# Converting half of the last part's weights inside the last part, and carrying W_out's second half through DRAM

## The chip, the cores and the metric

The kernel runs on one core of one Trainium2 chip. The metric is device time in microseconds (us), smaller is better. Three runs of the kernel before gave 1499.52, 1499.49 and 1498.40 us; their median, 1499.49 us, is the time to compare with. The profile is of one further execution.

## The reference, cut to what matters

Batch 8, 8 heads, sequence 576, head size 64, 32 memory slots; the weights and inputs arrive as 64-bit floats.

```
a = softmax of phi along the sequence
k_m, v_m = a^T k, a^T v                       # 32 memory slots for each head
x = softmax(q k_m^T / 8) v_m                  # 4608 tokens x 512
h = x @ w_in                                  # 512 -> 2048
x = (h - tanh(h)) @ w_out                     # 2048 -> 512
out = max(x @ w1, x @ w2, x @ w3) @ moe2_w_out   # 512 -> 768 -> 512
```

## The kernel before, in words

**Three stages.** The program computes the attention together with the tanh layer, and then the layer of three maxima, which is called the last part here. The tanh layer is cut into 16 blocks of 128 hidden units (`fc`). Blocks 0 to 7 are phase 0 and blocks 8 to 15 phase 1. In each phase the loop runs over tiles of 288 to 512 tokens, and within a tile over 8 blocks. One pass of that loop is a **step**: `emit_h` multiplies into PSUM (`ps_h`), `emit_g` makes `gh` = h - tanh(h) as a high and a low half (ScalarE `th`, VectorE L434, ScalarE cast L436, GpSimd L437), and `emit_x` multiplies `gh` by a block `wo` of W_out into `ps_x`, 12 matmuls. Phase 0 has 104 steps, phase 1 has 96; two batches take 24 steps of phase 1, and 24 of phase 0 after its first 32. The partial result goes to DRAM (`xd[0]`), and phase 1 adds its own share. Attention runs in the shadow of phase 0: generators for batches 2 to 7 are queued with due steps.

**Products.** Each product is three matmuls of high and low halves (`mm3`, L94 to L96), so each weight is needed as two 32-bit halves.

**Conversions.** `conv` (L113 to L138) turns 128 rows of 64-bit weights into those halves. It is one DMA into `raw` (two buffers), one ScalarE operation (L120), five VectorE operations (L122, L123, L125, L127, L128), one GpSimd addition (L134), one ScalarE cast into the high half (L135) and one GpSimd subtraction into the low half (L137). For w_in there is one half only, and one GpSimd addition (L131) ends it.

**What sets the order.** Two tracks (`Track`) hold generators, `fg` for attention and `bg` for conversions. `slot()` is called five times in a step and advances each track by `rate` quarters of a generator's step. An entry may have a gate, the first step at which it may move. On top of that the program's scheduler puts the instructions of each engine in an order of its own, so a conversion can stand earlier in an engine's queue than its place in the source. Every engine and each DMA queue works its instructions in that order.

**Which conversions stand where before the change.** W_out's blocks 0 to 7 and the first two quarters of w_in are converted at the start. The last part's weights (`last_w`: 24 pieces of W1 to W3 of 384 columns by `wb_conv`, 6 pieces of the last W_out by `wz_conv`) are converted from the first due step of batch 2 on, into one staging buffer `cs` (one copy only), and stored to DRAM: three DMAs for each `wb_conv` (L333), one for each `wz_conv` (L339). When attention is over and its memory is free, the third quarter of w_in (`wi2`) and W_out's blocks 8 to 15 (`wo1`) are converted, then the rest of `last_w`. In phase 1 the first two of six weight tiles `wb[j]` are loaded from DRAM (L591, GpSimd's queue), and at the start of the last part the other four (L608) and the six tiles `wz[j]` (L612).

**The last part.** Nine tiles of 512 tokens. For each, six groups `j`: `emit_max` runs 36 matmuls into three PSUM banks, ScalarE copies the first out (L624), VectorE takes two maxima (L625, L626), ScalarE and GpSimd split the result (`mh`, L628, L629). Each bank name has two buffers. From the second tile on `emit_out` is mixed in, 18 matmuls `ps_o` over all six `wz` for 128 tokens of the tile before. `split_x` prepares the next tile's input (`xr`, `xh`, L581, L582).

Of the kernel before, what the change touches and what calls it, by code (L numbers as in the profile page):

```python
# [22 lines left out]
def kernel(  # L23
# [26 lines left out]
    P = 128  # L50
# [62 lines left out]
    def conv(src, n, hi, lo=None):  # L113
        raw = cv_p.tile([P, 512, 2], U32, tag="raw", bufs=2, name="raw")
        DMA.dma_start(out=raw[:, :n].rearrange("p c t -> p (c t)"), in_=src.bitcast(U32))
        yield
        a = cv_p.tile([P, 512], U32, tag="cva", bufs=2, name="cva")[:, :n]
        b = cv_p.tile([P, 512], U32, tag="cvb", bufs=2, name="cvb")[:, :n]
        hw, lw = raw[:, :n, 1], raw[:, :n, 0]
# [205 lines left out]
    wb_d = [dram.tile([P, 3, KD, 2, P], F32, name=f"wb_d{j}") for j in range(J)]
    wz_d = [dram.tile([P, 2, DM], F32, name=f"wz_d{j}") for j in range(J)]

    def wb_conv(w, kc, g):
        t = cv_p.tile([P, 2, 512], F32R, tag="cs", bufs=1, name="cs")
# [4 lines left out]
        yield  # L334

    def wz_conv(j):
        t = cv_p.tile([P, 2, 512], F32R, tag="cs", bufs=1, name="cs")
        yield from conv(moe2_w_out[j * P:(j + 1) * P, :], DM, t[:, 0], t[:, 1])
        DMA.dma_start(out=wz_d[j], in_=f(t))  # L339
        yield  # L340
# [202 lines left out]
    for g in last_w:  # L543
        bg.add("last", g, start[0, 2])
# [68 lines left out]
    m_t = {}  # L613

    def emit_max(i, j):
# [7 lines left out]
        m = b_p.tile([P, NT], F32, tag="m", bufs=3, name="m")  # L623
# [8 lines left out]
    def emit_out(i, u):  # L632
        ps = ps_b.tile([P, DM], F32, tag="o", bufs=2, name="ps_o")
# [4 lines left out]
        ob = b_p.tile([P, DM], F32, tag="ob", bufs=3, name="ob")  # L638
# [50 lines left out]
```

## Time and profile before

| | before |
|---|---|
| median of three runs | 1499.49 us |
| the profiled execution | 1499.77 us |
| its span, first to last instruction | 1498.0 us |
| TensorE matmul (PE) busy | 1369.6 us, 91% |
| VectorE (DVE) busy | 645.1 us, 43% |
| GpSimd (POOL) busy | 461.5 us, 31% |
| ScalarE (ACT) busy | 419.8 us, 28% |
| mean granted TensorE clock | 0.975 |

PE is the matmul row, PEld its weight loads. A wait row says which engine's line waited for what: total us, how often, and the longest. SP issues most DMAs. "Landing" is the time from a DMA's issue to its completion.

The order of stages in the span is: start to 134 us, attention with phase 0 to 559, phase 1 to 897, the last part to the end.

### The profile page before, as it was taken

To read this page: it belongs to the slowest core of one execution; us is meant where nothing else is said; L and a number is where in the kernel's file an instruction comes from. 1 tells how busy PE (TensorE), PEld (TensorE's weight loads), DVE (VectorE), ACT (ScalarE), POOL (GpSimd) and SP (SyncE) were. 2 spreads that over 40 slices of the span, in tenths; PEclk is the share of its full clock that TensorE was granted. 3 is DMA by queue.
4 is the path that set the end of the run, shared out by engine and by line. 5 is a ranking of instruction groups with operands and counts; after the bars stand their busy time and mean duration, and the time that the engine had idled before them with its cause. 6 is when DMAs were issued, how large, how long until landed. Compare 5 with 4: busy or idle time off the path is not lost.

```text
span 1498.0 us, 21579 instructions
## 1 busy us (share of the span) xinstructions
PE 1369.6 (91%) x8672; PEld 1131.2 (76%) x8672; DVE 645.1 (43%) x1043; ACT 419.8 (28%) x817; POOL 461.5 (31%) x420
## 2 busy tenths in 40 slices
PE   2575988889998888999999999999999999999998
PEld 1354867677786666788898998888888888888887
DVE  3888787875447994642323222211212121211111
ACT  1323344343343353442323322111111111111110
POOL 0446555543335574543232332111111111111110
PEclk9977899999999998999999999999999999999999
DMA  8565878766432346642312227101101010110001
GB/s 208 142 192 142 230 214 233 210 173 162 120 118 79 129 157 207 209 155 78 113 47 85 75 73 272 36 15 46 46 14 43 15 47 17 43 35 15 15 14 43
DMA packets 190068, 159.75 MB, mean 107 GB/s; under 512 B 95248, under 2 KB 163856, under 8 KB 188176
## 3 DMA queue, kind: packets, MB, share of 16 engines
q1 hardware_dynamic: 188240, 145.79, 33.5%
q0 software_dynamic: 1728, 12.58, 2.3%
q8 instruction: 68, 1.11, 0.3%
q14 instruction: 32, 0.26, 0.1%
HBM read 105.64 MB, written 52.69 MB: 106 GB/s over the span
## 4 chain that ended last, share of the span: by engine, by line
PE 66%; DVE 13%; DMA 8%; SPq 5%; issue 3%; POOL 3%; ACT 2%; DVEq 0%; ACTq 0%; POOLq 0%
PE ps_w L96 10%; PE ps_w L95 10%; PE ps_w L94 10%; PE ps_x L94 5%; PE ps_x L95 5%; PE ps_x L96 5%; DMA wb_d<-cs 3%; PE ps_o L95 3%; PE ps_o L94 3%; PE ps_o L96 3%; PE ps_h L94 3%; PE ps_h L96 3%; PE ps_h L95 3%; DVE cvb L125 2%; SPq L176 2%
## 5 line engine op out<-in xcount | busy, mean ns | idle before, releaser
L437 POOL TENSOR_TENSOR gh<-th,gh 128x320 fp32r<-128x320 f32 (+2 forms) x200 | 209.7, 1050 | 320.3 <-ACT gh L436 311.4
L95 PE MATMUL ps_x<-gh,wo 128*128 128x320 f32 (+2 forms) x800 | 271.0, 341 | 6.7 <-POOL gh L437 6.5
L94 PE MATMUL ps_x<-gh,wo 128*128 128x320 f32 (+2 forms) x800 | 257.0, 343 | 11.8 <-ACT gh L436 6.6
L96 PE MATMUL ps_x<-gh,wo 128*128 128x320 f32 (+2 forms) x800 | 265.6, 335 | 0.7 <-POOL wo L137 0.7
L96 PE MATMUL ps_w<-xh,wb 128*128 128x512 f32 x648 | 255.0, 394 | 0.0
L95 PE MATMUL ps_w<-xh,wb 128*128 128x512 f32 x648 | 254.5, 393 | 0.0
L94 PE MATMUL ps_w<-xh,wb 128*128 128x512 f32 x648 | 253.9, 392 | 0.0
L629 POOL TENSOR_TENSOR mh<-m,mh 128x512 fp32r<-128x512 f32 x54 | 69.8, 1295 | 490.3 <-ACT mh L628 490.3
L434 DVE TENSOR_TENSOR th<-ps_h,th 128x320 f32<-128x320 f32 (+2 forms) x200 | 106.4, 534 | 197.8 <-ACT th L433 197.7
L94 PE MATMUL ps_h<-at,vw 128*128 128x320 f32 (+2 forms) x512 | 160.1, 313 | 32.5 <-DVE th L434 20.9
L94 PEld LDWEIGHTS ps_x<-gh,wo 128*128 128x128 f32 x800 | 150.8, 194 | 38.9 <-issue 17.7
L95 PEld LDWEIGHTS ps_x<-gh,wo 128*128 128x128 f32 x800 | 154.5, 193 | 27.9 <-POOL gh L437 14.5
L96 PEld LDWEIGHTS ps_x<-gh,wo 128*128 128x128 f32 x800 | 153.8, 193 | 10.9 <-issue 1.0
L625 DVE TENSOR_TENSOR m<-ps_w,m 128x512 f32<-128x512 f32 x54 | 37.3, 691 | 283.0 <-PE ps_w L96 283.0
L96 PE MATMUL ps_h<-at,vw 128*128 128x320 f32 (+2 forms) x512 | 155.5, 305 | 1.0 <-DVE vw L312 1.0
L95 PE MATMUL ps_h<-at,vw 128*128 128x320 f32 (+2 forms) x512 | 155.1, 303 | 0.0
L94 PEld LDWEIGHTS ps_h<-at,vw 128*128 128x128 f32 x512 | 100.4, 196 | 62.7 <-DVE th L434 35.6
L436 ACT CAST gh<-th 128x320 fp32r<-128x320 f32 (+2 forms) x200 | 99.7, 499 | 162.4 <-DVE th L434 150.6
L433 ACT ACTIVATE th<-ps_h 128x320 f32<-128x320 f32 (+2 forms) x200 | 94.8, 476 | 177.1 <-PE ps_h L96 168.8
L95 PEld LDWEIGHTS ps_w<-xh,wb 128*128 128x128 f32 x648 | 121.7, 188 | 27.8
L94 PEld LDWEIGHTS ps_w<-xh,wb 128*128 128x128 f32 x648 | 121.8, 188 | 27.5
L96 PEld LDWEIGHTS ps_w<-xh,wb 128*128 128x128 f32 x648 | 121.7, 188 | 27.1
(80 smaller groups left out, 1714.5 us busy)
## 6 DMA issues: line engine op xcount, KB each, us to landing
raw<-in_moe_w_out_dram SPq DMA_DIRECT2D x22, 512.0 KB, 3.5
qt<-in_q_dram SPq DMA_DIRECT2D x128, 72.0 KB, 3.0
at_d<-at SPq DMA_DIRECT2D x16, 576.0 KB, 3.5
raw<-in_moe_w_dram SPq DMA_DIRECT2D x24, 384.0 KB, 3.4
wb_d<-cs SPq DMA_DIRECT2D x72, 128.0 KB, 3.6
at<-at_d SPq DMA_DIRECT2D x8, 1152.0 KB, 5.6
wb<-wb_d POOLq DMA_DIRECT2D x6, 1536.0 KB, 9.3
xr<-xd SPq DMA_DIRECT2D x36, 256.0 KB, 2.9
```

The lines of the kernel that those rows point to most:

```text
L94: T.matmul(o, w[0], x[0], start=start, stop=False)
L95: T.matmul(o, w[0], x[1], start=False, stop=False)
L96: T.matmul(o, w[1], x[0], start=False, stop=stop)
L125: V.scalar_tensor_tensor(out=b, in0=hw, scalar=0xC0000000, in1=b, op0=ALU.bitwise_and, op1=ALU.bitwise_or)
L176: DMA.dma_start(out=t[64 * e + 32 * h:64 * e + 32 * h + 32, r], in_=src[e, h, r])
L433: S.activation(th, ps, AF.Tanh)
L434: V.tensor_sub(th, ps, th)
L436: S.copy(gh[:, 0], th)
L437: G.tensor_sub(gh[:, 1], th, f(gh[:, 0]))
L625: V.tensor_max(m, pss[1], m)
L629: G.tensor_sub(mh[:, 1], m, f(mh[:, 0]))
```

## The change

- `conv` loses the column count (it always takes 512 columns, now also as 4 x 128 of three-dimensional sources) and gets one `yield` more behind its DMA. Its buffers come from `cv[0]`, which is the last part's pool `b_p` once that is open.
- `wo_store` and `wo_load` are new: W_out's blocks 8 to 15 are converted from the first due step of batch 2 on, stored to DRAM (8 DMAs of 512 KB), and loaded into `wo1` when attention's memory is free.
- `wb_conv` takes one weight matrix and one `j` at a time, 512 x 128 entries. For j = 0 to 2 (nine conversions) it stages through `cs` and stores one DMA each, gated to phase 1. For j = 3 to 5 (nine) and for all six `wz` it writes straight into the last part's tiles while that part runs: `emit_max` steps the track six times ahead of each of its three products and then insists on what it needs.
- Of the loads at the start of the last part, one (`wb[2]`) stays. `m` and `ob` go from three to two buffers.

```diff
+    cv = [cv_p]
+    def conv(src, hi, lo=None):
+        raw = cv[0].tile([P, 512, 2], U32, tag="raw", bufs=2, name="raw")
...
+        yield
         yield
...
+    def wo_store(fc):
+        t = cv_p.tile([P, 2, DM], F32R, tag="cs", bufs=1, name="cs")
+        yield from conv(moe_w_out[(FC + fc) * P:(FC + fc + 1) * P, :], t[:, 0], t[:, 1])
+        DMA.dma_start(out=wo_d[fc], in_=f(t))
+        yield
+    def wo_load(fc):
+        t = wo_t[FC + fc] = wo1.tile([P, 2, DM], F32R, name=f"wo{FC + fc}")
+        DMA.dma_start(out=f(t), in_=wo_d[fc])
+        yield
+    JP = 3
+    def wb_conv(w, j, t=None):
+        o = cv_p.tile([P, KD, 2, P], F32R, tag="cs", bufs=1, name="cs") if t is None else t[:, w]
         src = (moe2_w1, moe2_w2, moe2_w3)[w]
-        yield from conv(src[kc * P:(kc + 1) * P, g * 384:(g + 1) * 384], 384, t[:, 0, :384], t[:, 1, :384])
-        for i in range(3):
-            DMA.dma_start(out=wb_d[3 * g + i][:, w, kc], in_=f(t[:, :, i * P:(i + 1) * P]))
+        yield from conv(src[:, j * P:(j + 1) * P].rearrange("(k p) c -> p k c", p=P), o[:, :, 0], o[:, :, 1])
+        if t is None:
+            DMA.dma_start(out=wb_d[j][:, w], in_=f(o))
+            yield
+    def wz_conv(j, t):
+        yield from conv(moe2_w_out[j * P:(j + 1) * P, :], t[:, 0], t[:, 1])
...
-    for g in last_w:
-        bg.add("last", g, start[0, 2])
+    for fc in range(FC):
+        bg.add("wos", wo_store(fc), start[0, 2])
...
-    bg.add("wo1", chain(*[wo_conv(fc, wo1) for fc in range(8, 16)]))
-    bg.q += rest
-    rate[1] = 8
+    bg.add("wo1", chain(*[wo_load(fc) for fc in range(FC)]))
+    for j in range(JP):
+        for w in range(3):
+            bg.add("wb", wb_conv(w, j), start[1, 0])
+    rate[1] = 6
...
+        if j < JP:
+            G.dma_start(out=wb[j], in_=wb_d[j])
+        else:
+            for w in range(3):
+                bg.add(("wb", j), wb_conv(w, j, wb[j]))
...
-        G.dma_start(out=wz[j], in_=wz_d[j])
+        bg.add("wz", wz_conv(j, wz[j]))
...
+        bg.need_all(("wb", j))
         for w in range(3):
+            for _ in range(LR):
+                bg.step(10 ** 9)
```

On VectorE, from the end of phase 1 into the last part, the kernel before has only the split of the next tile and the maxima (L465 is the last addition of phase 1, L582 the split, L625 and L626 the maxima):

```order
L465 TENSOR_TENSOR xo<-ps_x_8574,xo 128x320
L582 TENSOR_TENSOR xh<-xr,xh 128x512 x2
L625 TENSOR_TENSOR m<-ps_w_8799,m 128x512
L626 TENSOR_TENSOR m<-ps_w_8812,m 128x512
L625 TENSOR_TENSOR m<-ps_w_8845,m 128x512
L582 TENSOR_TENSOR xh<-xr,xh 128x512 x2
L626 TENSOR_TENSOR m<-ps_w_8858,m 128x512
```

In the changed kernel the same stretch of VectorE (L485, L602, L654 and L655 are now these lines; L126 to L132 are the five operations of a conversion):

```order
L485 TENSOR_TENSOR xo<-ps_x_8234,xo 128x320
L126 TENSOR_SCALAR cva<-cva 128x512
L127 TENSOR_SCALAR cvb<-cva 128x512
L129 SCALAR_TENSOR_TENSOR cvb<-raw,cvb 128x512
L126 TENSOR_SCALAR cva<-cva 128x512
L131 TENSOR_SCALAR cva<-cvb 128x512
L127 TENSOR_SCALAR cvb<-cva 128x512
L132 SCALAR_TENSOR_TENSOR cva<-raw,cva 128x512
L129 SCALAR_TENSOR_TENSOR cvb<-raw,cvb 128x512
L654 TENSOR_TENSOR m<-ps_w_8470,m 128x512
L602 TENSOR_TENSOR xh<-xr,xh 128x512 x2
```

Fifteen conversions, 75 such rows, stand between the end of phase 1 and the ninth pair of maxima.

On GpSimd, around the change from phase 0 to phase 1, the kernel before (L134 and L137 end a conversion, L437 is the step's own work, L591 the loads of `wb[0]` and `wb[1]`):

```order
L137 TENSOR_TENSOR wo_5465<-cva,wo_5465 128x512
L437 TENSOR_TENSOR gh<-th,gh 128x320
L134 TENSOR_TENSOR cva<-cvb,cva 128x384
L437 TENSOR_TENSOR gh<-th,gh 128x320
L137 TENSOR_TENSOR cs<-cva,cs 128x384
L134 TENSOR_TENSOR cva<-cvb,cva 128x384
L437 TENSOR_TENSOR gh<-th,gh 128x320
L591 DMA wb_5717<-wb_d_97 128x3072
L591 DMA wb_5718<-wb_d_98 128x3072
L134 TENSOR_TENSOR cva<-cvb,cva 128x384
L137 TENSOR_TENSOR cs<-cva,cs 128x384
```

The same place in the changed kernel (L138 and L142 end a conversion, L457 is the step's own work, L611 the loads):

```order
L142 TENSOR_TENSOR cs<-cva,cs 128x4x128
L138 TENSOR_TENSOR cva<-cvb,cva 128x512
L457 TENSOR_TENSOR gh<-th,gh 128x320 x2
L138 TENSOR_TENSOR cva<-cvb,cva 128x512
L142 TENSOR_TENSOR cs<-cva,cs 128x4x128
L611 DMA wb_5336<-wb_d_105 128x3072
L457 TENSOR_TENSOR gh<-th,gh 128x320 x3
L142 TENSOR_TENSOR cs<-cva,cs 128x4x128
```

The eight W_out conversions ahead of this place are gone, conversions of W1 to W3 stand there instead, staged through `cs`, and the two loads stand apart: `wb[1]` follows seven rows further down.

On ScalarE at the start of the last part the changed kernel has (L124 begins a conversion, L653 copies the first bank of a group out of PSUM, L140 casts a converted weight, L601 and L657 are the other casts):

```order
L124 ACTIVATE cva<-raw 128x512
L653 COPY m<-ps_w_8447 128x512
L124 ACTIVATE cva<-raw 128x512
L601 CAST xh<-xr 128x512 x2
L140 CAST wb_8428<-cva 128x4x128
L657 CAST mh<-m 128x512
L653 COPY m<-ps_w_8522 128x512
L140 CAST wb_8428<-cva 128x4x128
L124 ACTIVATE cva<-raw 128x512
```

The kernel before has L624, L581 and L628 there alone. The third conversion's first operation now stands behind the copy of the second group's first bank.

## Rows read from the trace of the kernel before

**Rows 1.** Windows: length; PE, PEld, DVE, ACT, POOL busy (count); clock; DMA share, GB/s

```profile
134.00:239.00 105.00, 89.66 (x890) 77.56 (x890) 82.88 (x150) 42.76 (x96) 59.10 (x59) 0.89 0.76 217
239.00:344.00 105.00, 94.00 (x896) 77.45 (x897) 80.91 (x135) 45.16 (x92) 55.92 (x52) 1.00 0.68 184
344.00:445.00 101.00, 96.62 (x956) 81.46 (x956) 54.32 (x94) 37.56 (x75) 35.38 (x33) 1.00 0.51 134
...
481.00:559.00 78.00, 66.20 (x369) 50.19 (x368) 74.01 (x96) 31.83 (x63) 50.03 (x40) 1.00 0.40 134
559.00:657.00 98.00, 88.91 (x548) 74.47 (x547) 57.73 (x97) 40.32 (x83) 51.22 (x46) 0.95 0.63 211
657.00:740.00 83.00, 83.00 (x539) 71.91 (x538) 23.65 (x44) 27.32 (x55) 24.38 (x24) 1.00 0.26 90
682.00:740.00 58.00, 58.00 (x364) 49.61 (x362) 15.99 (x29) 18.28 (x37) 16.54 (x16) 1.00 0.29 100
897.00:1498.00 601.00, 596.18 (x2596) 486.97 (x2594) 109.38 (x162) 92.83 (x158) 74.01 (x62) 1.00 0.15 46
```

**Rows 2.** Windows of the tile ps_x alone: PE, PEld, DVE, ACT busy (matmuls)

```profile
481.00:559.00 78.00, 41.43 (x192) 31.90 (x192) 1.35 (x2) 1.55 (x4) 1.00 0.40 134
...
682.00:740.00 58.00, 39.74 (x192) 31.85 (x192) 4.17 (x8) 0.00 (x0) 1.00 0.29 100
```

**Rows 3.** Waits of ACT, 130 to 345 and 445 to 660: total, times, longest

```profile
ACT cs L135 <- DMA wb_d<-cs: 36.6, 16, 5.1
...
ACT cs L135 <- DMA wb_d<-cs: 15.4, 3, 8.7
```

**Rows 4.** Groups by line and form, DVE, 481 to 559: busy us, mean ns

```profile
L125 DVE SCALAR_TENSOR_TENSOR cvb<-raw,cvb 128x512 uint32<-128x512 uint32 x13 | 15.7, 1211 | 0.3
L128 DVE SCALAR_TENSOR_TENSOR cva<-raw,cva 128x512 f32<-128x512 uint32 x13 | 10.8, 835 | 0.3
L127 DVE TENSOR_SCALAR cva<-cvb 128x512 uint32<-128x512 uint32 x13 | 10.6, 816 | 0.3
L123 DVE TENSOR_SCALAR cvb<-cva 128x512 uint32<-128x512 uint32 x12 | 10.5, 874 | 0.3
L122 DVE TENSOR_SCALAR cva<-cva 128x512 f32<-128x512 f32 x12 | 8.9, 739 | 2.6 <-ACT cva L120 2.6
```

**Rows 5.** The tiles cva and cvb, whole span: min/median/max ns

```profile
L122 DVE TENSOR_SCALAR cva<-cva x62: 343/428/1420, 30.0 to 632.3; 128x512 f32<-128x512 f32 x38, 128x384 f32<-128x384 f32 x24
L123 DVE TENSOR_SCALAR cvb<-cva x62: 301/426/1637, 30.4 to 633.0; 128x512 uint32<-128x512 uint32 x38, 128x384 uint32<-128x384 uint32 x24
...
L125 DVE SCALAR_TENSOR_TENSOR cvb<-raw,cvb x62: 503/691/1784, 30.9 to 634.6; 128x512 uint32<-128x512 uint32 x38, 128x384 uint32<-128x384 uint32 x24
L127 DVE TENSOR_SCALAR cva<-cvb x62: 341/426/1407, 32.2 to 635.6; 128x512 uint32<-128x512 uint32 x38, 128x384 uint32<-128x384 uint32 x24
L128 DVE SCALAR_TENSOR_TENSOR cva<-raw,cva x62: 508/692/1787, 32.9 to 636.7; 128x512 f32<-128x512 uint32 x38, 128x384 f32<-128x384 uint32 x24
```

**Rows 6.** Timeline of POOL and of DVE, 505 to 509: start, duration

```profile
506.41 1.47 POOL L134 TENSOR_TENSOR cva<-cvb,cva 128x512 f32<-128x512 f32 x1
...
506.77 1.40 DVE L123 TENSOR_SCALAR cvb<-cva 128x512 uint32<-128x512 uint32 x1
```

**Rows 7.** Groups by form, POOL and ACT, 481 to 559

```profile
L137 POOL TENSOR_TENSOR wo<-cva,wo 128x512 fp32r<-128x512 f32 x8 | 11.5, 1434 | 1.5 <-ACT wo L135 1.5
L134 POOL TENSOR_TENSOR cva<-cvb,cva 128x512 f32<-128x512 f32 x8 | 10.7, 1338 | 8.7 <-DVE cva L128 8.7
...
L135 ACT CAST wo<-cva 128x512 fp32r<-128x512 f32 x8 | 5.0, 619 | 6.2 <-POOL cva L134 6.1
```

**Rows 8.** Groups by form, DVE and POOL, the last part, 897 to the end

```profile
L625 DVE TENSOR_TENSOR m<-ps_w,m 128x512 f32<-128x512 f32 x54 | 37.3, 691 | 283.0 <-PE ps_w L96 283.0
...
L629 POOL TENSOR_TENSOR mh<-m,mh 128x512 fp32r<-128x512 f32 x54 | 69.8, 1295 | 490.3 <-ACT mh L628 490.3
```

**Rows 9.** DMA issues, whole span: KB each, median us to landing

```profile
wz_d<-cs SPq DMA_DIRECT2D x6, 512.0 KB, 3.1
```

More of the change, by code (lines that the diff above doesn't have):

```diff
@@ L110, in small @@
             tc.add_manual_dep(b, a.name, mybir.DependencyInfo(mybir.DependencyClass.NoSync, mybir.DependencyReason.DATA), reason="side by side")
[L113 to L115 removed]
+    cv = [cv_p]
+    def conv(src, hi, lo=None):
+        raw = cv[0].tile([P, 512, 2], U32, tag="raw", bufs=2, name="raw")
+        u = src.bitcast(U32)
+        DMA.dma_start(out=raw.rearrange("p (k c) t -> p k (c t)", k=u.shape[1]) if len(u.shape) == 3 else raw.rearrange("p c t -> p (c t)"), in_=u)
         yield
[L117 to L119 removed]
+        yield
+        a = cv[0].tile([P, 512], U32, tag="cva", bufs=2, name="cva")
+        b = cv[0].tile([P, 512], U32, tag="cvb", bufs=2, name="cvb")
+        hw, lw = raw[:, :, 1], raw[:, :, 0]
         S.activation(f(a), f(hw), AF.Abs)
@@ L134, in conv @@
         G.tensor_add(f(a), f(b), f(a))
-        S.copy(hi, f(a))
+        x = f(a).rearrange("p (k c) -> p k c", k=hi.shape[1]) if len(hi.shape) == 3 else f(a)
+        S.copy(hi, x)
         yield
-        G.tensor_sub(lo, f(a), f(hi))
+        G.tensor_sub(lo, x, f(hi))
         yield
@@ L145, in wi_conv @@
         for r in range(HP):
-            yield from conv(moe_w_in[r * P:(r + 1) * P, fq * FQ:(fq + 1) * FQ], FQ, t[:, r])
+            yield from conv(moe_w_in[r * P:(r + 1) * P, fq * FQ:(fq + 1) * FQ], t[:, r])
         wi[fq] = t
@@ L320, in wo_conv @@
         t = p.tile([P, 2, DM], F32R, name=f"wo{fc}")
-        yield from conv(moe_w_out[fc * P:(fc + 1) * P, :], DM, t[:, 0], t[:, 1])
+        yield from conv(moe_w_out[fc * P:(fc + 1) * P, :], t[:, 0], t[:, 1])
         wo_t[fc] = t
[L325 to L329, printed above, removed]
-        src = (moe2_w1, moe2_w2, moe2_w3)[w]
-        yield from conv(src[kc * P:(kc + 1) * P, g * 384:(g + 1) * 384], 384, t[:, 0, :384], t[:, 1, :384])
-        for i in range(3):
-            DMA.dma_start(out=wb_d[3 * g + i][:, w, kc], in_=f(t[:, :, i * P:(i + 1) * P]))
[L334 to L340, printed above, removed]
+    wo_d = [dram.tile([P, 2, DM], F32, name=f"wo_d{fc}") for fc in range(FC)]
+    def wo_store(fc):
[8 more added lines that the diff above has]
+    JP = 3
+    wb_d = [dram.tile([P, 3, KD, 2, P], F32, name=f"wb_d{j}") for j in range(JP)]
+    def wb_conv(w, j, t=None):
+        o = cv_p.tile([P, KD, 2, P], F32R, tag="cs", bufs=1, name="cs") if t is None else t[:, w]
+        src = (moe2_w1, moe2_w2, moe2_w3)[w]
+        yield from conv(src[:, j * P:(j + 1) * P].rearrange("(k p) c -> p k c", p=P), o[:, :, 0], o[:, :, 1])
[4 more added lines that the diff above has]
+        yield from conv(moe2_w_out[j * P:(j + 1) * P, :], t[:, 0], t[:, 1])
     class Track:
@@ L366, in need, with need_all @@
                         break
+        def need_all(self, name):
+            while any(x[0] == name for x in self.q):
+                self.need(name)
     fg, bg = Track(), Track()
@@ L622, in emit_max @@
             pss.append(ps)
-        m = b_p.tile([P, NT], F32, tag="m", bufs=3, name="m")
+        m = b_p.tile([P, NT], F32, tag="m", bufs=2, name="m")
         S.copy(m, pss[0])
@@ L637, in emit_out @@
             mm3(ps, (mh[:, 0, o], mh[:, 1, o]), (wz[j][:, 0], wz[j][:, 1]), j == 0, j == J - 1)
-        ob = b_p.tile([P, DM], F32, tag="ob", bufs=3, name="ob")
+        ob = b_p.tile([P, DM], F32, tag="ob", bufs=2, name="ob")
         (S.copy if u % 2 else V.tensor_copy)(ob, ps)
```

8 lines of the change are left out of this document (4 added, 4 removed).

## The prediction

> **What bounds the kernel now.** I read the windows by stage first: in which stretch is PE (TensorE's matmul row) short of the stretch, and which engine is full there. From 897 to the end PE is busy 596.2 of 601 us at full clock [rows 1]. The last part is bound by its matmuls, so nothing taken from it is worth anything there, and whatever makes PE wait adds to the time. In phase 1, once the conversions are over, PE is busy 83.0 of 83.0 us for 24 steps (657 to 740), and 58.0 of 58.0 for the 16 steps from 682 [rows 1]. These two are my floors. The stretches that are longer than their floors all hold conversions:
>
> - 481 to 559, the last 16 steps of phase 0, takes 78 us. It has the same 192 matmuls into `ps_x` as the 58 us from 682 [rows 2]. DVE (VectorE) is busy 74.0 of the 78 [rows 1]: it is the bound.
> - 559 to 657, the first 24 steps of phase 1, takes 98 us against 83, with the granted clock at 0.95 [rows 1]. The waits of ACT (ScalarE) show one of 8.7 us for the store of `cs` [rows 3]; it stands beside the loads of `wb[0]` and `wb[1]`.
> - 239 to 344 takes 105 us, 344 to 445 takes 101 [rows 1], both for 24 steps with two batches of attention. The first holds ten conversions, the second none. So with attention beside them the conversions cost 4 us in 105, not more.
>
> **What one conversion costs.** On DVE between 481 and 559 the five operations average 1.211, 0.835, 0.816, 0.874 and 0.739 us [rows 4], together 4.5 us. Their medians over the whole span are 0.43, 0.43, 0.69, 0.43 and 0.69, together 2.7 [rows 5]. The difference is waiting for POOL (GpSimd): a 0.43 us operation that starts at 506.77 takes 1.40 us and ends about when POOL's addition of 506.41 ends [rows 6]. POOL itself spends 1.34 + 1.43 = 2.8 us on a conversion [rows 7].
>
> **The change, stretch by stretch.** The conversions stay the same number of weights: 62 before (24 of them of 384 columns), 56 after, all of 512. What matters is where they stand on DVE.
>
> 1. *134 to 344, gain 6 us (0 to 10).* The instruction order has 9 conversions where 12 stood up to 239, and 2 where 10 stood from 239 to 344. For the second piece the difference between the two equal stretches bounds the gain at 4 us [rows 1]; I take 3. In the first piece DVE has the same work within a few us, since 512 columns cost more than 384; what falls away is two thirds of the stores of `cs`. ACT waited 16 times, 36.6 us in all, for them between 130 and 345 [rows 3], with `th` and `gh` of the coming steps queued behind. I take 3.
> 2. *481 to 559, gain 10 us (4 to 16).* There are 12 conversions in these steps instead of 15: the eight of W_out are now loads, six of W1 to W3 move in from later, and of w_in two have their DVE part done long before. Three at 4.5 us are 13.4 us off a DVE that is 95% busy; the floor, 58 us, is not reached. I take back 3 us, because the six go through the one `cs`: cast 0.6 and subtraction 1.4 [rows 7], landing 3.1 [rows 9] and the issue ahead of it make between 5 and 6 us each, in some 40 us. The eight new loads of W_out, 4 MB, sit in SP's queue right behind attention's last store near 480 and are needed from 559 on. At 3.1 us for a transfer of that size [rows 9] they take 25 us even one after the other, and are there about 50 us early: nothing.
> 3. *559 to 657, gain 9 us (2 to 14).* Of the 15 us over the floor 8.7 are that one wait, and 0.05 of 98 us, about 5, the lower clock. After the change a store of `cs` still stands directly ahead of the load of `wb[0]`, but `wb[1]` comes seven rows later, so half as many bytes stand in the way at once: I leave half of the wait and none of the clock's loss. Three or four conversions follow here instead of nine or ten.
> 4. *657 to 897: nothing.* No conversion stood here and none does now.
> 5. *The last part, loss 11 us (0 to 25).* Fifteen conversions now run beside matmuls that have no slack. Its 2592 matmuls take 601 us [rows 1], 0.232 each, so a group `j` takes PE 36 x 0.232 = 8.35 us. In the changed order the product that needs the last converted tile comes after 343 matmuls, 79.6 us into the part, near 976.9. DVE starts after phase 1's last additions, near 898.3, and has before it: 15 x 4.475 = 67.1 us of conversions, 16 maxima at 0.691 [rows 8] = 11.1, four splits of about the same length = 2.8, and about 5 us of waiting for `xr`'s DMA and for ACT at the start. That is 984.3; POOL's addition, ACT's cast and POOL's subtraction add 3.4, so 987.7. PE waits 10.8 us in all. I take the 4.5 us because POOL is about as busy as between 481 and 559, where it was 50.0 of 78 [rows 1]: 15 x 2.8 plus eight `mh` at 1.295 [rows 8] are 52 in 88 us. The tail's 3.4 us are 1.34, 0.62 and 1.43 [rows 7]. At 2.7 us a conversion is hidden, that is the low end. If DVE and POOL took strict turns, 2.7 + 2.8 = 5.4 us, it would be 81.5 for the conversions, 10.4 for `mh`, 2.8, 5 and 3.4 on top of 898.3, so 24.5 us late: the high end. ACT, busy 92.8 of the 601 us [rows 1], has room for its two operations a conversion, and three loads of `wb` and six of `wz` fall away from POOL's queue; they were hidden.
> 6. *The clock, loss 2 us (0 to 8).* With PE idle 11 of 105 us the granted clock stayed at 1.00 (239 to 344), with 15 of 105 it was 0.89 [rows 1]. Some 11 us of waiting spread over 80 lies between.
>
> Sum: -6 - 10 - 9 + 11 + 2 = -12 us on the profiled execution's 1499.8, 1487.8. The median is 0.3 us lower, so I say **1487 us**.
>
> A rule speaks against point 5. The Trainium skill, "SBUF — State Buffer", section "Who interferes with whom", says that GpSimd and certain VectorE operations (two-port modes, or two inputs in SBUF) hold a shared port pair exclusively, so that the second "fully blocks" for the whole instruction. The 1.40 us operation [rows 6] agrees with it. By it alone point 5 would be near the high end, 25 us, and the sum 1501; the average of 4.5 us between 481 and 559 [rows 4] says that only part of the operations collide.
>
> **The rivals.**
>
> - *Hidden, 1474 us.* DVE and POOL collide less than between 481 and 559, a conversion takes about 3.5 us, and PE waits under 2 us; the gains reach 27. For it: in the last part POOL has no `gh` every 3 to 5 us. Against it: POOL's share comes out the same.
> - *Strict turns, 1501 us, no change.* The two engines alternate, 5.4 us a conversion, the last part loses 25 and the clock 2, which eats the gain of 25. For it [rows 6]; against it the average [rows 4].
> - *The conversions never were the bound, 1499 us, no change.* Points 1 to 3 give half, 12 us, since `cs` still has one buffer and `wb[0]` still stands beside its store; the last part loses 13. For it: 101 against 105 us; against it: DVE at 95% from 481.
> - *Slower, 1508 us: conversions and products hold each other up in ACT's queue.* The third conversion's first operation stands behind the copy of a PSUM bank that waits for PE, and PE soon waits for weights. Each wait of the one then stretches the other, and the pace falls to 5.8 us or more. From 5.5 us on the change loses: (5.5 - 4.475) x 15 is 15 us on top of 13 and passes the 25 gained by more than the noise. At 5.8 the last part loses 31; with the clock at 0.97 in 80 us, 2 more, 33 - 25 = +8.
>
> **How the numbers follow.** Forecast (1478 to 1496) 0.46; hidden 0.20; strict turns 0.10; no bound 0.10; slower 0.14. A measurement tells about 0.2%, 3 us, from no change. Faster: 0.46 + 0.20 and 0.02 of the third rival, 0.68. Same: 0.07 of the third and 0.06 of strict turns, 0.13. Slower: 0.14, with 0.04 of strict turns and 0.01 of the third, 0.19. The range 1466 to 1508 leaves out one in ten at each end: a hidden last part with the gains near their high ends (40 us) below, and a lock with the lower gains above. The forecast's own range is 1478 to 1496.
>
> **What would show it.** Right: the last 16 steps of phase 0 near 68 us with DVE under 90%; the first 24 of phase 1 near 89 with no wait over 5 us for `cs`; the last part 605 to 620 us instead of 601, with PE waiting for POOL's L142 or ACT's L140 between 925 and 990 of the old time and not later, and conversions at 4 to 5 us on DVE there. Wrong: a last part under 603 us or over 626, conversions at 5.5 us or more, or the stretches of points 2 and 3 unchanged.

## The result, and the profile after

The changed kernel takes 1465.42 us (median of four runs, 1464.11 to 1466.06) against 1499.51 beside it: ratio 0.9773, 95% interval 0.9756 to 0.9790, so 34 us less. The forecast was 1487 with a range from 1466 to 1508. The direction was right and the size wrong: the gain is nearly three times the 12 us forecast. The profiled execution took 1464.11 us, its span is 1462.4.

I cut both spans at the first `ps_x` matmul of the same steps. In us (steps 0 to 103 are phase 0, 104 to 199 phase 1):

| steps | before | after | change | forecast |
|---|---|---|---|---|
| 0-8 | 69.5 | 63.3 | -6.2 | 0 |
| 8-32 | 104.5 | 100.5 | -4.0 | -3 |
| 32-56 | 104.8 | 93.9 | -10.9 | -3 |
| 56-88 | 137.8 | 138.1 | +0.3 | 0 |
| 88-104 | 77.7 | 62.3 | -15.5 | -10 |
| 104-128 | 97.7 | 85.2 | -12.5 | -9 |
| 128-199 | 238.6 | 238.4 | -0.2 | 0 |
| last part | 601 | 613 | +12.3 | +13 |

Windows of the changed kernel, with the columns of [rows 1], in the order 8-32, 32-56, 56-80, 88-104, 104-128, the 16 steps that answer to 682:740, and the last part:

```profile
129.00:230.00 101.00, 88.92 (x895) 74.63 (x894) 85.10 (x142) 41.46 (x93) 55.73 (x53) 0.94 0.77 230
230.00:324.00 94.00, 90.90 (x897) 77.73 (x897) 52.99 (x94) 37.91 (x74) 38.40 (x35) 1.00 0.49 136
324.00:425.00 101.00, 97.62 (x955) 82.76 (x954) 54.63 (x93) 38.41 (x77) 36.05 (x33) 0.98 0.51 134
...
462.00:524.00 62.00, 59.76 (x358) 49.04 (x356) 48.42 (x75) 27.01 (x55) 36.49 (x30) 1.00 0.61 214
524.00:609.00 85.00, 85.00 (x550) 73.07 (x544) 38.86 (x64) 34.30 (x69) 37.89 (x36) 1.00 0.51 176
...
634.00:692.00 58.00, 58.00 (x366) 49.63 (x362) 15.93 (x29) 18.37 (x37) 16.53 (x16) 1.00 0.28 101
849.00:1462.00 613.00, 600.54 (x2596) 489.13 (x2594) 170.49 (x237) 109.88 (x187) 113.05 (x84) 0.99 0.15 43
```

Read the fourth row, steps 88 to 104, against [rows 1]: DVE was busy 74.0 of 78 us and is busy 48.4 of 62. PE went from 66.2 of 78 to 59.8 of 62. In the fifth, steps 104 to 128, PE is never idle: 85.0 of 85.

ACT's waits for the store of `cs`, which stood at 36.6 and 15.4 us in [rows 3]. First steps 8 to 56, then 104 to 128:

```profile
ACT cs L140 <- DMA wo_d<-cs: 13.6, 5, 3.8
...
ACT cs L140 <- DMA wb_d<-cs: 5.6, 2, 2.8
```

All of the 15.4 us stood in steps 104 to 128. What PE felt of them in the kernel before (559.2 to 657) was one wait for `gh`, which ACT makes; in the changed kernel PE waits for nothing there:

```profile
PE ps_x L94 <- ACT gh L436: 6.6, 1, 6.6
```

PE's waits between 860 and 960, where the last part now loses. They are all it has in the last part for converted weights:

```profile
PE ps_w L94 <- ACT wb L140: 3.5, 2, 2.7
PE ps_o L94 <- ACT wz L140: 3.4, 1, 3.4
PE ps_o L95 <- POOL wz L142: 1.0, 1, 1.0
```

From the start of one matmul to the start of the next, four gaps there are 1.1 us (at 885.6), 3.1 (891.8), 3.8 (924.95) and 1.4 (938.8). That is 9.4 in all, or 8.5 beyond the 0.23 us that a matmul takes itself. Twice, soon after a long gap, the granted clock is at its lower level (1.2 of 2.4 GHz) for about 3.4 us, which costs about 3.4 us in all:

```profile
894.00:899.00 5.00, 4.02 (x11) 3.24 (x12) 4.97 (x6) 2.56 (x4) 3.64 (x4) 0.66 0.49 165
928.00:933.00 5.00, 4.29 (x12) 3.40 (x13) 4.93 (x9) 1.92 (x3) 1.93 (x3) 0.66 0.53 181
```

Together that is 11.9 of the 12.3 us in the table. VectorE's groups in the fifteen conversions, 849 to 940:

```profile
L129 DVE SCALAR_TENSOR_TENSOR cvb<-raw,cvb 128x512 uint32<-128x512 uint32 x15 | 14.4, 958 | 0.4
L127 DVE TENSOR_SCALAR cvb<-cva 128x512 uint32<-128x512 uint32 x15 | 13.7, 910 | 0.3
L131 DVE TENSOR_SCALAR cva<-cvb 128x512 uint32<-128x512 uint32 x15 | 12.3, 818 | 0.3
L126 DVE TENSOR_SCALAR cva<-cva 128x512 f32<-128x512 f32 x15 | 12.2, 813 | 8.4 <-ACT cva L124 5.6 <-POOL mh L658 2.8
L132 DVE SCALAR_TENSOR_TENSOR cva<-raw,cva 128x512 f32<-128x512 uint32 x15 | 11.4, 758 | 0.3
```

The means add up to 4.26 us a conversion; the forecast took 4.475. The trace also shows what lengthens them. I sorted these 75 operations by whether one of GpSimd's runs beside them for more than 0.05 us. The 38 that meet none take 0.41 to 0.43 us (L126, L127, L131) or 0.67 to 0.69 (L129, L132), which adds up to 2.6 us a conversion. The 37 that meet one take 0.42 to 1.79 us, 1.16 on average. So the whole distance from 2.6 to 4.26 us stands beside GpSimd's operations, and about half of the operations meet one.

### The profile page after: what moved, and what is told of

Same layout as the page of the kernel before. It is cut to its first block, busy times and chain, and to the rows that moved or that the text cites. A ratio compares the mean times of both kernels' runs of the same rounds, so it can differ in the third digit from the quotient of the medians.

```text
span 1462.4 us, 21348 instructions
## 1 busy us (share of the span) xinstructions
PE 1359.7 (93%) x8672; PEld 1128.9 (77%) x8672; DVE 637.0 (44%) x1013; ACT 418.6 (29%) x805; POOL 450.9 (31%) x399
## 4 chain that ended last, share of the span: by engine, by line
PE 72%; DVE 12%; DMA 5%; SPq 4%; issue 3%; POOL 2%; ACT 1%; DVEq 0%; POOLq 0%; ACTq 0%
PE ps_w L96 9%; PE ps_w L95 9%; PE ps_w L94 9%; PE ps_x L94 7%; PE ps_x L95 7%; PE ps_x L96 7%; PE ps_h L94 4%; PE ps_h L96 4%; PE ps_h L95 4%; PE ps_o L95 3%; PE ps_o L96 3%; PE ps_o L94 3%; SPq L181 2%; PE ps_w L106 2%; DVE cvb L129 2%
## 5 line engine op out<-in xcount | busy, mean ns | idle before, releaser
L457 POOL TENSOR_TENSOR gh<-th,gh 128x320 fp32r<-128x320 f32 (+2 forms) x200 | 204.3, 1023 | 348.0 <-ACT gh L456 329.2
L94 PEld LDWEIGHTS ps_x<-gh,wo 128*128 128x128 f32 x800 | 148.7, 191 | 37.4 <-issue 17.8
L95 PEld LDWEIGHTS ps_x<-gh,wo 128*128 128x128 f32 x800 | 152.4, 190 | 18.9 <-issue 7.2
L96 PEld LDWEIGHTS ps_x<-gh,wo 128*128 128x128 f32 x800 | 152.0, 190 | 11.0 <-issue 0.9
L654 DVE TENSOR_TENSOR m<-ps_w,m 128x512 f32<-128x512 f32 x54 | 37.3, 690 | 246.2 <-PE ps_w L96 246.2
```

The costliest lines, as they stand in the source:

```text
L94: T.matmul(o, w[0], x[0], start=start, stop=False)
L95: T.matmul(o, w[0], x[1], start=False, stop=False)
L96: T.matmul(o, w[1], x[0], start=False, stop=stop)
L457: G.tensor_sub(gh[:, 1], th, f(gh[:, 0]))
L654: V.tensor_max(m, pss[1], m)
```

## The experiments

The ratios are to the kernel before, run beside each. The table gives, in us, the stretches in which each kernel differs, from its profile. Within attention one profile is good to a few us only, as the runs of one kernel spread by up to 11 us.

| run | 0-8 | 8-56 | 56-88 | 88-104 | 104-128 | 128-199 | last part | ratio (interval) |
|---|---|---|---|---|---|---|---|---|
| before | 69.5 | 209.3 | 137.8 | 77.7 | 97.7 | 238.6 | 601 | 1 |
| after | 63.3 | 194.4 | 138.1 | 62.3 | 85.2 | 238.4 | 613 | 0.9773 (0.9756-0.9790) |
| e1 | 67.1 | 200.8 | 137.4 | 74.1 | 93.8 | 245.3 | 601 | 0.9919 (0.9891-0.9948) |
| e2 | 64.6 | 202.8 | 145.4 | 78.2 | 101.9 | 238.6 | 601 | 0.9998 (0.9983-1.0013) |
| e3 | 64.4 | 193.4 | 138.6 | 66.8 | 85.1 | 238.4 | 613 | 0.9787 (0.9752-0.9822) |
| e4 | 63.8 | 195.6 | 138.3 | 63.2 | 93.7 | 245.3 | 601 | 0.9802 (0.9774-0.9830) |
| e5 | 63.7 | 196.1 | 138.5 | 57.7 | 85.0 | 239.6 | 601 | 0.9652 (0.9638-0.9667) |
| e6 | 69.4 | 211.8 | 138.6 | 75.6 | 89.0 | 238.0 | 601 | 0.9927 (0.9912-0.9942) |
| e7 | 68.6 | 200.6 | 139.4 | 62.5 | 85.2 | 238.4 | 613 | 0.9814 (0.9794-0.9834) |
| e8 | 63.1 | 193.9 | 138.8 | 63.4 | 85.2 | 238.4 | 611 | 0.9750 (0.9730-0.9771) |
| e9 | 64.5 | 194.5 | 138.3 | 57.7 | 85.0 | 239.6 | 601 | 0.9653 (0.9625-0.9681) |

### e1: fewer conversions beside attention

```diff
-    for g in last_w:
-        bg.add("last", g, start[0, 2])
+    for n, g in enumerate(last_w):
+        bg.add("last", g, start[0, 2] if n < 12 else start[1, 0])
-    bg.q, rest = bg.q[:1], bg.q[1:]
+    bg.q, rest = [], bg.q
```

> The kernel before, with the last 18 of the 30 conversions of the last part's weights held until phase 1. The order then has 3 conversions in steps 32 to 56 where 10 stood; steps 88 to 104 keep 14 of their 15. Theory A (conversions cost PE time wherever attention already fills VectorE): steps 32 to 56 fall from 105 us to 93 to 96. Theory B (my prediction's: attention alone sets about 101 us for 24 steps with two batches): they stay at 100 to 102. Both: steps 88 to 104 stay at 75 to 78 us. The held conversions go into steps 104 to 137; if VectorE has room there, the total falls by 9 us under A (about 1490) and by 4 under B (about 1495); if each held conversion costs there what it costs before, the total stays at 1499.

Steps 32 to 56 fell from 104.8 to 97.0 us, a us above theory A's range and well below B's. The floor of 101 that I took from the stretch 344 to 445 is none: theory B fell. The held conversions took 6.7 us of the gain back in steps 128 to 199, and the total came to 1488.33. The trace before could have told it, had I cut it by tiles. Windows of the kernel before, steps 32 to 40, 40 to 48, 48 to 56, 56 to 64, 64 to 72 and 72 to 80:

```profile
238.90:265.70 26.80, 23.22 (x179) 20.85 (x179) 22.53 (x41) 12.20 (x25) 16.86 (x15) 1.00 0.77 191
265.70:313.40 47.70, 42.61 (x396) 31.88 (x394) 39.65 (x61) 18.38 (x36) 25.43 (x23) 1.00 0.74 195
313.40:343.70 30.30, 27.95 (x324) 24.53 (x322) 18.68 (x34) 14.59 (x32) 13.56 (x14) 1.00 0.51 164
343.70:378.70 35.00, 30.62 (x253) 25.91 (x250) 23.74 (x40) 12.88 (x27) 12.66 (x12) 1.00 0.66 172
378.70:417.70 39.00, 39.00 (x384) 30.68 (x383) 19.51 (x33) 12.51 (x23) 12.51 (x12) 1.00 0.51 122
417.70:444.50 26.80, 26.80 (x325) 24.66 (x325) 10.79 (x21) 11.93 (x25) 10.28 (x11) 1.00 0.29 96
```

The fifth and sixth are PE from end to end: a tile of 512 tokens takes 39.0 us there, one of 320 takes 26.8, so by estimate 24 steps (320, 512 and 320 tokens) can be done in 92.6. It is an estimate because the tiles do not hold equal shares of attention's matmuls. The loss of the stretch 344 to 445 is in its first tile alone (35.0). The changed kernel's steps 32 to 56 take 93.9.

### e2 and e7: the extra yield alone, and the change without it

```diff
         DMA.dma_start(out=raw[:, :n].rearrange("p c t -> p (c t)"), in_=src.bitcast(U32))
         yield
+        yield
```

> The kernel before, with nothing but the extra yield behind the load of each conversion. The changed kernel lost 6 us in steps 0 to 8, where neither staging nor the last part plays a part, so theory A is that the yield alone gives it: steps 0 to 8 fall from 69.5 to about 63 us and the total to about 1493. Theory B: it comes from elsewhere, steps 0 to 8 stay at 69 to 70, the total within 3 us of 1499. On steps 32 to 56 (10 conversions as before) both expect 104 to 106.

> The changed kernel without the extra yield behind a conversion's load. Theory A (the yield gives what steps 0 to 32 won): steps 0 to 8 go back from 63.3 to 68 to 70 us and steps 8 to 32 from 100.5 to 103 to 105, total 1472 to 1476. Theory B (the gain of those steps is the order of W_out's conversions, and the yield only happens to give the like): they stay at 63 to 65 and 99 to 102, total 1463 to 1467. Both: steps 88 to 128 and the last part as in the changed kernel, 62, 85 and 613 us.

The yield is what changed steps 0 to 8: put into the kernel before, it takes them from 69.5 to 64.6 us; taken out of the changed kernel, they go back to 68.6, and steps 8 to 32 to 104.5. It acts by the order of attention's own operations. In steps 0 to 8 PE and VectorE work in the same order in e7 as in the kernel before. e12 to e15 below have no yield, but the scheduler gave them another order there too, and their steps 0 to 8 take 63.9 to 65.6 us. So the yield found a better order; it is not needed for one.

e2's stretch went as theory A had it, its total as theory B: steps 56 to 64 take 42.9 us instead of 35.0 and steps 104 to 128 4.2 more. In the changed kernel, where few conversions are left from step 40 on, the gain stays: e7 took 1473.96 us, as theory A had it. By the ratios the yield is worth 6 us there, by the profiles 10.

### e3 and e4: each half of the change undone

```diff
-    for fc in range(FC):
-        bg.add("wos", wo_store(fc), start[0, 2])
+    for j in range(JP):
+        for w in range(3):
+            bg.add("wb", wb_conv(w, j), start[0, 2])
...
-    bg.add("wo1", chain(*[wo_load(fc) for fc in range(FC)]))
+    bg.add("wo1", chain(*[wo_conv(fc, wo1) for fc in range(8, 16)]))
```

> The changed kernel with its W_out part undone: blocks 8 to 15 of W_out converted after attention, straight into their tiles, the nine staged conversions of W1 to W3 during attention as before. The fifteen in the last part stay. Theory A (the number of conversions in a stretch decides): steps 32 to 56 as in the changed kernel, 94 to 96 us; steps 88 to 104 with 13 conversions straight into tiles 64 to 70; last part 613; total 1463 to 1473. Theory B (taking W_out through DRAM is what frees steps 88 to 104): these take 74 to 78 us, total 1476 to 1482.

Theory A. Without W_out's way through DRAM only steps 88 to 104 differ clearly, 66.8 against 62.3 us (62.5 to 63.4 in e4, e7 and e8, which have the same W_out part). Beside the other half this half is worth 4.5 us in these steps; the totals, 0.9787 and 0.9773, are too close to tell it.

The other half undone (JP = 6; `wz` staged through `cs`, stored and loaded as before; rate 3 in phase 1):

> The changed kernel with its last-part half undone: all 24 conversions of the last part's weights in phase 1, staged, stored and loaded as before the change; 18 of them stand in steps 104 to 138 instead of 3. Last part 600 to 602 us in both theories. Theory A (phase 1 has room on VectorE for a conversion every other step, the 98 us of the kernel before came from the two tile loads beside a store and from the conversions left over from attention): steps 104 to 138 lose at most 4 us, total 1452 to 1457. Theory B (conversions in the first steps of phase 1 cost about a us each, as 11 of them did before, 98 us against 83): steps 104 to 138 lose 13 to 18, total 1464 to 1471.

Theory B by the numbers: steps 104 to 128 went from 85.2 to 93.7 and 128 to 199 from 238.4 to 245.3, together 15.4 us for fifteen more conversions, more than the last part got back. The median, 1471.32, stands 0.3 us above its range. VectorE was not full in steps 104 to 128, the third figure behind the length here:

```profile
527.00:620.00 93.00, 88.35 (x543) 72.56 (x542) 73.60 (x104) 41.39 (x82) 58.75 (x51) 1.00 0.74 256
```

ACT's waits between 526 and 655 point elsewhere:

```profile
ACT cs L140 <- DMA wb_d<-cs: 22.2, 10, 4.4
```

So does the chain that ended last, 622 to 637: the cast waits for the store of the conversion before it, and that store for that conversion's own last operations.

```profile
622.84 5.51 DMA wb_d<-cs
628.35 0.02 issue
628.37 0.63 ACT cs L140
...
629.12 1.31 POOL cs L142
630.45 5.90 DMA wb_d<-cs
```

### e5: the same conversions, three steps apart

A gate in the source is not enough, since the scheduler may put a conversion earlier: of the changed kernel's nine conversions with a gate at step 104 (524.0 us), five have their cast before it, the first at 491.3. So this kernel adds an order on ACT, behind the tanh of a given step:

```diff
-        S.activation(f(a), f(hw), AF.Abs)
+        first = S.activation(f(a), f(hw), AF.Abs).ins
+        if at is not None:
+            tc.add_manual_dep(first, th_ins[at].name, mybir.DependencyInfo(mybir.DependencyClass.NoSync, mybir.DependencyReason.DATA), reason="held")
...
+            g = start[1, 0] + 3 * (3 * j + w)
+            bg.add("wb", wb_conv(w, j, at=g), g)
```

> The kernel of the run with all 24 conversions in phase 1, but each conversion's first ScalarE operation now ordered behind the tanh of step 104, 107, 110 and so on to 173, one every three steps, so that the store of the staging buffer before it (5 to 6 us) is over when the cast needs the buffer. Steps 88 to 104 keep 6 conversions. Theory A (a conversion costs PE about 1 us by its VectorE and GpSimd time, wherever it stands): steps 104 to 199 take 321 us plus 15 to 24, total about 1465. Theory B (it costs by waiting for the one staging buffer, with the coming steps' operations queued behind on ScalarE): no wait over 1 us for a store of the staging buffer remains, steps 104 to 199 take 321 to 326 us, the last part 600 to 602, steps 88 to 104 58 to 62, total 1448 to 1454.

Theory B. 1451.52 us: 13 us below the changed kernel by the profiles, 18 by the ratios. From step 104 on one wait for a store of the staging buffer is left, of 1.3 us. Twenty-four conversions in phase 1 cost it nearly nothing: steps 104 to 199 take 324.5 us where the changed kernel, with three, takes 323.6. So in phase 1 VectorE's and GpSimd's work on a conversion has no price of its own. The price came with standing close together. That it was the wait for the one staging buffer is what e4's waits and chain say; spacing also thins out the engines' work, and no run here has a second staging buffer in phase 1, which would part the two. PE is busy from end to end from step 88 to the last part (windows of e5, steps 88 to 104, 104 to 128, 128 to 199, last part):

```profile
465.00:522.00 57.00, 57.00 (x358) 48.78 (x356) 32.30 (x52) 22.79 (x46) 24.48 (x22) 1.00 0.44 156
522.00:607.00 85.00, 85.00 (x552) 73.05 (x544) 51.39 (x88) 38.97 (x76) 47.15 (x43) 1.00 0.67 232
607.00:847.00 240.00, 240.00 (x1561) 213.39 (x1556) 113.86 (x198) 97.26 (x190) 115.19 (x104) 1.00 0.40 143
849.00:1449.00 600.00, 595.57 (x2592) 486.33 (x2590) 108.77 (x160) 92.84 (x158) 74.05 (x62) 1.00 0.15 46
```

### e8 and e9: the last part

e8 moves the addition of the fifteen conversions from GpSimd to VectorE:

```diff
-        G.tensor_add(f(a), f(b), f(a))
+        (G if cv[0] is cv_p else V).tensor_add(f(a), f(b), f(a))
```

> The changed kernel with one operation of the fifteen conversions in the last part moved: the addition of the two halves from GpSimd to VectorE, where the like operation takes 0.69 us alone. In the changed kernel VectorE spends 4.27 us on a conversion there, against 2.7 by the medians. Theory A (the 1.57 us between them is waiting for GpSimd's own operations, of which this takes away one of two): VectorE's six operations take 4.0 to 4.4 us in all, the last part stays at 610 to 615 us, total within 3 us of the changed kernel. Theory B (VectorE is slow there for a reason of its own): 4.27 + 0.69 = 4.96 us, fifteen of them end 10 us later, the last part takes 621 to 625, total about 1474.

```profile
L129 DVE SCALAR_TENSOR_TENSOR cvb<-raw,cvb 128x512 uint32<-128x512 uint32 x15 | 15.5, 1033 | 0.3
L132 DVE SCALAR_TENSOR_TENSOR cva<-raw,cva 128x512 f32<-128x512 uint32 x15 | 11.8, 788 | 0.3
L131 DVE TENSOR_SCALAR cva<-cvb 128x512 uint32<-128x512 uint32 x15 | 11.4, 763 | 0.2
L138 DVE TENSOR_TENSOR cva<-cvb,cva 128x512 f32<-128x512 f32 x15 | 11.2, 748 | 0.1
L126 DVE TENSOR_SCALAR cva<-cva 128x512 f32<-128x512 f32 x15 | 10.2, 681 | 3.0 <-ACT cva L124 2.8
L127 DVE TENSOR_SCALAR cvb<-cva 128x512 uint32<-128x512 uint32 x15 | 7.3, 485 | 0.2
```

Six operations take 67.4 us over fifteen conversions, 4.49 each: 0.23 more than five took, not the 0.69 of the added one. The other five fell from 4.26 to 3.75. The last part takes 611 us. So GpSimd's operations do lengthen VectorE's. The 4.49 lie just above theory A's range, since GpSimd keeps the subtraction and the split of `mh`: of the 90 operations 53 meet none of GpSimd's, and none of those takes more than 0.69 us.

e9 leaves nine conversions in the last part (JP = 5) and holds fifteen in phase 1 as in e5:

> The changed kernel with wb[3] and wb[4] taken out of the last part: 15 conversions of W1 to W3 in phase 1, held to one every three steps, and only wb[5] and the six tiles of the last W_out, nine conversions, in the last part. Theory A (the last part loses only where a tile is later than its first product: wb[5]'s three conversions have 40 us, all nine have 58 us for about 42 us of VectorE): PE waits under 1.5 us for weights, last part 602 to 604, total 1448 to 1454, as with all 24 in phase 1. Theory B (each conversion costs PE about 0.8 us wherever it stands beside the products, 12.3 for 15): last part 608 to 610, total 1456 to 1460.

Theory A: 601 us, and PE waits for no converted weight. Median 1450.97 us, the same as e5 within their intervals. A conversion in the last part costs nothing as long as its tile is not late. By estimate fifteen were two or three too many in that order: PE's 8.5 us of gaps are the VectorE time of two conversions, the loss of 12.3 that of three.

### e6, e10 to e15: what a conversion costs beside attention

e6 gives the kernel before a second staging buffer while attention runs:

```diff
+    def cs_tile():
+        turn[0] += 1
+        p = ap if turn[0] % 2 and now[0] < 80 else cv_p
+        return p.tile([P, 2, 512], F32R, tag="cs", bufs=1, name="cs")
```

> The kernel before with a second staging buffer while attention runs (and one kvn buffer instead of two, to make room). The order has 15 conversions in steps 8 to 32 instead of 12, and 7 in 32 to 56 instead of 10. Theory B (in attention too the one staging buffer costs the time): ScalarE's waits for the stores between steps 8 and 56 fall from 36.6 us to under 10, and these steps take 195 to 202 us instead of 209.3, total 1488 to 1493. Theory A (VectorE's and GpSimd's work costs it): the waits fall too, but the steps take 207 to 211 us, total 1497 to 1501.

ACT's waits for the stores between steps 8 and 56 fell from the 36.6 us of [rows 3] to this:

```profile
ACT cs L135 <- DMA wb_d<-cs: 7.0, 6, 1.8
```

and the steps took 211.8 us, none less, as theory A had it. The order changed with the edit: 16 conversions start in steps 8 to 32 instead of 12, so this is not the buffer alone. But my 3 us for fewer such waits (point 1) did not show. The total fell by 0.7%, into theory B's range and for another reason: nearly all of it is in steps 104 to 128, 89.0 against 97.7, where the longest wait for a store is 5.6 us and not 8.7.

e10 leaves VectorE's part out of ten conversions:

```diff
+        if light:
+            G.tensor_add(f(a), f(a), f(a))
+            S.copy(hi, f(a))
...
+            return
```

> The kernel before with the five VectorE operations left out of ten conversions (the 13th to 22nd of W1 to W3, whose values are then not the weights); their loads, ScalarE and GpSimd operations and stores stay. Nine of them stand in steps 40 to 53; one full conversion stands at 36, and the next two come at 54 and 56. Theory A (beside attention a conversion costs PE time by VectorE's share of it): steps 32 to 56 fall from 105 us to 94 to 98, nearly as with seven conversions held back. Theory B (by its loads, its GpSimd operations or ScalarE's waits for the staging buffer): they stay at 102 to 106. Both: steps 8 to 32 as before, 103 to 106, last part 601.

```profile
236.00:338.00 102.00, 94.99 (x890) 78.66 (x889) 55.25 (x97) 46.55 (x97) 57.33 (x56) 0.98 0.75 200
```

Steps 32 to 56 took 102.7 us with VectorE busy for 55 of 102 instead of 81 of 105, and steps 56 to 88 3.8 more. Theory A fell too. The total is 0.9910 (0.9884 to 0.9935), and most of that is in steps 104 to 128, 86.1 against 97.7, where six full conversions start instead of nine. e11 has both edits:

> The kernel of the run with ten conversions light (their five VectorE operations left out, so those weights are wrong), now with the second staging buffer of the other run beside it. Alone the light conversions left steps 8 to 56 at 207.3 us and the second buffer at 211.8, against 209.3 before and 200.8 with seven conversions held back. Theory C (two limits stand side by side, VectorE's work and the staging waits; whichever is taken away, the other remains): without both the steps take 196 to 202 us. Theory D (neither is the price; the loads beside attention's own or GpSimd's operations are): they stay at 205 to 210.

213.3 us for steps 8 to 56, ratio 0.9940 (0.9921 to 0.9959). Theory C fell, and the time is above D's range too. Left were the loads and the work on GpSimd and ScalarE. No run takes out GpSimd's. e12 adds seven loads to e1, each with one ScalarE operation:

```diff
+        raw = ap.tile([P, 384, 2], U32, tag="raw2", bufs=1, name="raw2")
+        DMA.dma_start(out=raw.rearrange("p c t -> p (c t)"), in_=src[:P, :384].bitcast(U32))
+        x = S.activation(f(raw[:, :, 0]), f(raw[:, :, 1]), AF.Abs).ins
```

> The kernel before with 18 conversions held until phase 1, as in the first run, plus seven loads of the same size as a conversion's into a buffer of their own between steps 40 and 53, each followed by one ScalarE operation of the conversion's size, and nothing else of a conversion. The first run took 200.8 us for steps 8 to 56, the kernel before 209.3. Theory C (VectorE's work and the staging waits are the price): 199 to 203. Theory D (the loads are: they stand in SP's queue and in the DMA engines beside attention's own loads): 206 to 210. Both: the stretches from step 88 on as in the first run, 74, 94 and 245 us.

207.9 us against e1's 200.8, ratio 0.9944 (0.9921 to 0.9968), where e1 had 0.9919 (0.9891 to 0.9948): by its profile theory D, by the totals not told apart from e1. Its controls:

> The kernel of the run with seven extra loads, with six of the seven loads left out and the seven ScalarE operations kept (they work on the one tile that is loaded). The order of everything else is the same. Theory D (the loads cost what conversions cost beside attention): steps 8 to 56 fall from 207.9 us to 199 to 203. Theory F (the loads cost nothing; the ScalarE operation, or the order of the conversions that the extra work shifted, is what cost 7 us): they stay at 205 to 210.

> The kernel of the run with seven extra loads, these loads issued from GpSimd's queue instead of SP's. Theory D1 (a load costs by its place in SP's queue, ahead of attention's loads of q, k, v and phi): steps 8 to 56 fall to 199 to 203 us. Theory D2 (it costs in the DMA engines and in memory, whichever queue it comes from): they stay at 206 to 210.

> The kernel of the run with seven extra loads, now fourteen, one a step from 40 to 53. Theory D (about a us for each load): steps 8 to 56 take 213 to 218 us. Theory F (the loads are not the price): 205 to 210.

Their profiles say 202.8 us without six of the seven loads, 203.7 with the loads on GpSimd's queue (near theory D1), and 210.5 with fourteen, which is nearer to theory F. But the totals don't bear out the first: e13's ratio is 0.9959 (0.9940 to 0.9978), no better than e12's, and its profile is the lowest of its eight runs (1489.5, median 1494.0). So the ScalarE operations, and the order that they shift, may cost as much as the loads seem to. The order is no small matter: in e12 to e15 attention's own operations stand otherwise than in e1 from step 0 on, and their steps 8 to 32 take 94.7 to 102.7 us and steps 32 to 56 take 101.0 to 115.8, against 103.8 and 97.0. e14's 0.9900 (0.9870 to 0.9931) overlaps e12's interval. e15, 0.9982 (0.9966 to 0.9997), is all but clear of e12's, and PE and VectorE work in e12's order up to step 56: seven more loads with their ScalarE operations probably do cost. What stays open is how the price of a conversion beside attention divides between its loads, their place in SP's queue, its work on GpSimd and ScalarE, and the order in which attention's own operations come.

## Why the prediction was right and wrong

- **Point 1, steps 32 to 56: the step that failed.** "With attention beside them the conversions cost 4 us in 105, not more" took a stretch without conversions for the floor. That stretch has a loss of its own, 8.2 us in its first tile, and the tiles behind it show a floor of 92.6. The eight conversions that left were worth 10.9 us here, not 3 (some 2 of it by the yield: e7 takes 96.1); e1, with seven fewer, got 7.8. Why one costs a us there stays open.
- **Point 1, up to step 32: the cause was wrong.** I gave 3 us to fewer stores of `cs`; e6 took most of those waits away and gained nothing. The 10 us of steps 0 to 32 come with the order that the extra yield brings (e7), which I had priced at nothing, without saying so; 6.2 of them stand in steps 0 to 8, which the sum does not have at all.
- **Point 2, mechanism right, size off: 15.5 us instead of 10.** The terms of the sum were too small. I counted three conversions fewer by the order, 12 for 15; in the trace it is 10 for 14. I held 4.5 us a conversion fixed, but by the means each fell from 4.5 to 3.7. So VectorE's work on them fell from 64.2 us to 37.3, by 26.9 and not 13.4. And the 3 us taken back for the staging were not lost: ACT waited 2.3 us there, once. Counted in the traces by the operation that writes `cvb` from `raw`, the conversions in steps 88 to 104 and the us are 5: 57.7 (e5), 10: 62.3 (after), 11: 66.8 (e3), 12: 74.1 (e1), 14: 77.7 (before). Up to ten they cost 0.9 us each, from there to fourteen 3.9 on average. A constant price per conversion was the wrong form. That VectorE is full explains only the last of them: it is busy 78% of the window in the changed kernel, 77% in e3, 84% in e1 and 95% in the kernel before. The last three convert W_out in these steps and the other two load it, and no run parts the kind from the number.
- **Point 3, mechanism right, size off: 12.5 instead of 9.** I left half of the 8.7 us wait. None was left that PE felt: the longest is 2.8 us and PE is busy 85.0 of 85, with the clock's 5 us back as well. Before, PE had felt 6.6 us of it in one wait. e4 puts the waits back and loses 8.5 us in these steps; e5, with eight conversions in them, has one wait of 1.3 us and no loss.
- **Point 4 right**, 0.2 us.
- **Points 5 and 6 right: 12.3 us instead of 13.** The last tile's last subtraction was forecast to end at 987.7, which is 939.8 on the new span (47.9 us earlier); it ended at 941.4. PE waits 8.5 us for 10.8, the clock costs 3.4 for 2. The waits name L140 and L142, as expected. That the end comes out so close is partly luck. The fifteen conversions take 63.9 us for the forecast's 67.1, but there are eight splits at 0.88 (7.0 us) for four at 0.69 (2.8), VectorE idles 8.4 us for 5, and its intervals in the trace overlap by 4.6.
- **The Trainium skill's rule** ("SBUF — State Buffer", "Who interferes with whom"), read as a lock on every operation, gave 25 us for the last part; the average decided, and 12.3 came out. The trace agrees with it for the operations that meet one of GpSimd's (37 of 75, 1.16 us on average) and shows why the average is lower: the other 38 meet none and are not lengthened.
- **The rivals.** None came. The one of conversions and products holding each other up in ACT's queue hardly shows: ACT waits 6.5 us for `ps_w` in all, and the pace was 4.26 us, not 5.8. The range missed by 0.6 us because it took the gains' high ends together for no more than 40 us; they were 47.9, of which steps 0 to 8, without a term, gave 6.2.

The change is a gain of 48 us ahead of the last part and a loss of 12 in it. Its halves do not add up. Either alone, with the yield, gives nearly all: 0.9787 with the in-place half (e3) and 0.9802 with W_out through DRAM (e4), against 0.9773 with both, as each by itself empties steps 32 to 56. Beside the in-place half W_out's way through DRAM wins 4.5 us in steps 88 to 104; beside that, the in-place half wins 15.4 in phase 1 and loses 12 in the last part. e5 does without it and is 13 us faster by the profiles, by spacing.

## What to carry to other kernels

A floor must come from a stretch in which the bounding engine is busy from end to end: cut a candidate by tiles before you call it one. Work put beside a bound stretch need not have a fixed price: here the first ten conversions of a stretch cost 0.9 us each and the next four 3.9, and 24 of them spaced out nearly nothing. Price it by what waits, and count in the trace, not in the order alone. Two halves of a change that clear the same stretch do not add up; test each alone. With one staging buffer, look whether the work comes closer together than its store takes to land; a gate in the source may not hold it apart, so look at the order that results.

## What the runs showed of the hardware

The same store of 512 KB from `cs` landed after 2.8 us (median) where the conversions stood three steps apart (e9, 520 to 606) and after 4.6 where they followed each other (e4, 526 to 655):

```profile
wb_d<-cs SPq DMA_DIRECT2D x8, 512.0 KB, 2.8
...
wb_d<-cs SPq DMA_DIRECT2D x14, 512.0 KB, 4.6
```

In the changed kernel's last part two gaps of PE, of 3.1 and 3.8 us from start to start, were each followed by some 3.4 us at the lower clock, while gaps of 1.1 and 1.4 us were not.

VectorE's operations of a conversion take 0.41 to 0.43 or 0.67 to 0.69 us where none of GpSimd's runs beside them, and 1.16 on average where one does (the changed kernel, 849 to 941). This holds for the one-input operations on 32-bit integers too: L131 takes 0.41 to 0.43 us nine times and 1.37 to 1.51 six times.
